# A linear-attention and rational feed-forward kernel: steps ordered by a whole-program table, loads held back, coefficients formed early

## Chip, cores, metric

One NeuronCore of one Trainium2 chip. The metric is the device time of one execution in microseconds, as the median of the runs; "span" is the length of the one profiled execution, some 1.5 to 2 us shorter. PE is TensorE, DVE VectorE, ACT ScalarE, POOL GpSimd, SP SyncE.

## The reference, cut to what matters

```python
# q, k, v, f_logit: (4, 8, 768, 48) float32
f = 1.0 / (1.0 + np.exp(-f_logit))
for t in range(S):
    state = f[:, :, t, :, None] * state + np.einsum('bhd,bhe->bhde', k[:, :, t], v[:, :, t])
    y[:, :, t] = np.einsum('bhd,bhde->bhe', q[:, :, t], state)
x = y.transpose(0, 2, 1, 3).reshape(3072, 384)
h = x @ w_in                                   # (3072, 2048)
P = a[0] + a[1] * h + a[2] * h**2 + a[3] * h**3
Q = 1.0 + np.abs(b[0]) * np.abs(h) + np.abs(b[1]) * h**2
out = (P / (Q + 1e-06)) @ w_out                # (3072, 384)
```

## The kernel before

The attention goes in chunks of 128 tokens; a *unit* is one chunk of two batches, 12 in all. Each unit feeds two *groups* of the feed-forward part (8 of 16 blocks of d_ff each), 24 groups in all. The order is set by hand: no scheduler reorders it, so each engine is given its instructions in the order in which the kernel names them. Steps: `a_ef` log of the gate, `a_cs` its running sum, `a_exp` the two decay factors A0 and A1, `a_mul` q and k times these, `a_T`/`a_Te` transposes and their copy (qkT), `a_sc`/`a_mask` scores, `a_sv`/`a_st` state, `a_y`/`a_ye` output, `a_x`/`a_xe` its transpose (xT); `m_h`/`m_y` h = x w_in and its cast, `m_sq`, `m_abs`, `m_u`, `m_ln`, `m_ex` the reciprocal of Q as exp(-ln), `m_p1` to `m_p3` the polynomial, `m_g` the product, `m_o`/`m_oe` the second matmul and its copy out.

```python
    def load(n):                      # one unit: f, k, q on SP's queue, v (cast to bf16) on GpSimd's
        ...
        for dst, src, eng in ((fn, f_logit, nc.sync), (kn, k, nc.sync),
                              (qn, q, nc.sync), (vn, v, nc.gpsimd)):
            for j in range(UB):
                eng.dma_start(out=dst[:, j], in_=src[...].rearrange("h t d -> t h d"))
# --- start (cut) ---
    a_mul(0)
    coefficients()
    for cast in casts:
        cast()
    load_w_in(2)
    load_w_in(3)
    load(2)
    ...
    load(3)
    for g in range(KF // WB):
        load_w_out(g)
# --- the loop, odd half period (cut) ---
            a_y(mf)
            a_ye(mf)
            if isu(mu):
                a_exp(mu, 1)
            m_u(gp_, 0)
            m_ln(gp_, 0)
            m_u(gp_, 1)
            m_ln(gp_, 1)
            a_st(mf)
            a_x(mf)
            a_xe(mf)
            if isu(mu):
                a_mul(mu)
                a_T(mu)
            m_ex(gp_)
            m_h(gh, 0)
            m_h(gh, 1)
            m_y(gh, 0)
            m_y(gh, 1)
            o_of(n, 0)
```

PSUM: a ring of two buffers for cs, hp (h) and u; one buffer for tp, scores and y; one each for the state and the op sums.

Of the kernel before, what the change touches and what calls it, by code (L numbers as in the profile page):

```python
# [14 lines left out]
PSUM = bass.MemoryType.PSUM  # L15


@with_exitstack
def kernel(
# [14 lines left out]
    C = 128  # L34
# [31 lines left out]

    U = consts.tile([C, C], BF16, name="U")
# [13 lines left out]
    sig = w_pool.tile([P, 4], F32, name="sig")  # L81
    w_in_sb = w_pool.tile([P, KD, d_ff], BF16, name="w_in_sb")
# [7 lines left out]
    def load(n):  # L90
        c, u = units[n]
        t0 = c * C
        fn = ld.tile([C, UB, H, D], F32, name="fn")
        kn = ld.tile([C, UB, H, D], F32, name="kn")
        qn = ld.tile([C, UB, H, D], F32, name="qn")
        vn = ld.tile([C, UB, H, D], BF16, name="vn")
        for dst, src, eng in ((fn, f_logit, nc.sync), (kn, k, nc.sync),
                              (qn, q, nc.sync), (vn, v, nc.gpsimd)):
            for j in range(UB):
                eng.dma_start(out=dst[:, j],  # L100
                              in_=src[u * UB + j, :, t0:t0 + C, :].rearrange("h t d -> t h d"))
        at_[n] = dict(fn=fn, kn=kn, qn=qn, vn=vn, qk=qkp[n % NQK], ls=lsp[n % NQK],
                      st=states[u], c=c, u=u)
# [23 lines left out]
    def a_mul(n):  # L127
        s = at_[n]
        nc.vector.tensor_mul(s["qk"][:, :, 0, :, 0:D], s["qn"], s["A", 0])  # L129
        nc.vector.tensor_mul(s["qk"][:, :, 1, :, 0:D], s["kn"], s["A", 1])  # L130
# [11 lines left out]

    def a_Te(n):
        s = at_[n]
        t = at.tile([P, UB, 2, HP, C], BF16, name="qkT")
        nc.vector.tensor_copy(t.rearrange("p j a b c -> p (j a b c)"),  # L146
                              s["tp"].rearrange("p j a b c -> p (j a b c)"))
        s["qkT"] = t
# [26 lines left out]
    def a_sc(n, j, ring=False):  # L175
        s = at_[n]
        sc = (psr if ring else psA).tile([C, 2, HP, C], F32, name="sc", tag="r" if ring else "A")
        for p in range(HP):
            for i in range(2):
                r = slice(64 * i, 64 * i + D)  # L180
                nc.tensor.matmul(sc[:, i, p, :], s["qkT"][r, j, 1, p, :], s["qkT"][r, j, 0, p, :],  # L181
                                 start=True, stop=True)
        s["sc", j] = sc
# [80 lines left out]

    def m_y(n, half):
        s = mg[n]
        if half == 0:
            s["y"] = ms.tile([P, W], BF16, name="hy")
        nc.scalar.copy(s["y"][:, half * W // 2:(half + 1) * W // 2],  # L269
                       s["hp", half].rearrange("p a n -> p (a n)"))  # L270
# [6 lines left out]
    def m_abs(n):  # L277
        s = mg[n]
        s["z"] = ms.tile([P, W], BF16, name="z")
        nc.vector.tensor_scalar(s["z"].bitcast(U16), s["y"].bitcast(U16), 0x7FFF, None,  # L280
                                op0=ALU.bitwise_and)
        m_u_early(n)
# [3 lines left out]
    def way_u(n):  # L286
        return "dve" if n >= NGR - 2 else "pe"

    def way_p(n):
        return "dve" if n >= NGR - 2 else "dma"  # L290

    def m_u(n, half):
        s = mg[n]
        way = way_u(n)
        if way == "pe":
            u = psr.tile([P, 2, NB], F32, name="u", tag="r")
            for i, src in enumerate((s["h2"], s["z"])):
                for e in range(2):
                    nc.tensor.matmul(u[:, e, :], ident,  # L299
                                     src[:, (half * 2 + e) * NB:(half * 2 + e + 1) * NB],  # L300
                                     start=(i == 0), stop=(i == 1))
            s["u", half] = u
        elif half == 0:
            m_u_early(n)

    def m_u_early(n):
        s = mg[n]
        if "u" in s:
            return
        s["u"] = s["z"]  # L310
        if way_u(n) == "dve":
            nc.vector.tensor_add(s["z"], s["z"], s["h2"])
        elif way_u(n) == "dma":
            nc.gpsimd.dma_start(out=s["z"], in_=s["h2"], accum_op=ALU.add)
        else:
            del s["u"]

    def m_ln(n, half):
        s = mg[n]
        if half == 0:  # L320
            s["lq"] = ms.tile([P, W], F32, name="lq", bufs=1)
        if ("u", half) in s:
            nc.scalar.activation(s["lq"][:, half * W // 2:(half + 1) * W // 2],  # L323
                                 s["u", half].rearrange("p a n -> p (a n)"), AF.Ln,
                                 scale=sig[:, 2:3], bias=1.0 + 1e-6)
        elif half == 0:
            nc.scalar.activation(s["lq"], s["u"], AF.Ln, scale=sig[:, 2:3], bias=1.0 + 1e-6)

    def part_of(t, part, parts):
        return t[:, part * W // parts:(part + 1) * W // parts]  # L330

    def m_ex(n, part=0, parts=1):
        s = mg[n]
        if part == 0:
            s["qi"] = ms.tile([P, W], BF16, name="qi")
        nc.scalar.activation(part_of(s["qi"], part, parts), part_of(s["lq"], part, parts), AF.Exp, scale=-1.0)  # L336

    def m_p1(n):

        s = mg[n]  # L340
        s["t"] = ms.tile([P, W], BF16, name="t", bufs=3)
        nc.vector.tensor_scalar(s["t"], s["y"], a_sb[:, 3:4], a_sb[:, 2:3], op0=ALU.mult, op1=ALU.add)
        nc.vector.tensor_mul(s["t"], s["t"], s["h2"])  # L343

    def m_p2(n):
        s = mg[n]
        s["pb"] = ms.tile([P, W], BF16, name="pb")
        nc.vector.tensor_scalar(s["pb"], s["y"], a_sb[:, 1:2], a_sb[:, 0:1], op0=ALU.mult, op1=ALU.add)  # L348

    def m_p3(n):  # L350
        s = mg[n]
        if way_p(n) == "dma":
# [31 lines left out]
    def m_oe(m, b, eng=None, queue=None):  # L384
        c, u = units[m]
        osb = ms.tile([P, DM], F32, name="osb", bufs=4)
        if eng is nc.vector:
            nc.vector.tensor_copy(osb, ops.pop((m, b)))
        else:
            nc.scalar.copy(osb, ops.pop((m, b)))  # L390
# [15 lines left out]
    def load_w_out(g):  # L406
        nc.gpsimd.dma_start(out=w_out_sb[:, g * WB:(g + 1) * WB, :],
                            in_=moe_w_out[g * WB * P:(g + 1) * WB * P, :].rearrange("(ko ki) n -> ki ko n", ki=P))


    load(0)
    nc.sync.dma_start(out=b_sb, in_=bass.AP(tensor=moe_b.tensor, offset=moe_b.offset,
                                            ap=[[0, P]] + list(moe_b.ap)))
    nc.sync.dma_start(out=a_sb, in_=bass.AP(tensor=moe_a.tensor, offset=moe_a.offset,
                                            ap=[[0, P]] + list(moe_a.ap)))
    make_upper_triangular(nc, U, 1.0, diag=True)
    make_identity(nc, ident)
    nc.vector.memset(zeros, 0.0)
# [10 lines left out]

    make_upper_triangular(nc, mask, 1.0, diag=True)  # L430
    casts = [load_w_in(0, False), load_w_in(1, False)]
    load(1)
# [13 lines left out]
    def isg(n):  # L446
        return 0 <= n < NGR

    def isu(m):
        return 0 <= m < NUN  # L450

    def o_of(n, part):

        m, b = divmod(n - NG - 1, NG)
        half = KF // 2
        if 0 <= m < NUN - 1:
            m_o(m, b, range(part * half, (part + 1) * half))

    def oe_of(n):
        m, b = divmod(n - NG - 1, NG)  # L460
        if 0 <= m < NUN - 1:
            m_oe(m, b)


    busy(12)
    a_ef(0)
    a_cs(0)
    a_exp(0, 0)
    a_exp(0, 1)
    a_mul(0)  # L470
    coefficients()
    for cast in casts:
        cast()
    load_w_in(2)
    load_w_in(3)
    load(2)
    busy(14)
    a_T(0)
    busy(6)
    a_Te(0)  # L480
    a_sc(0, 0)
    a_sc(0, 1, ring=True)
    a_sv(0)
    busy(3)
    a_al(0)
    a_mask(0, 0)
    a_mask(0, 1)
    a_y(0)
    busy(6)
    a_ye(0)  # L490
    a_st(0)
    a_x(0)
    busy(6)
    a_xe(0)
    a_ef(1)
    a_cs(1)
    m_h(0, 0)
    m_y(0, 0)
    a_exp(1, 0)
    m_h(0, 1)  # L500
    a_exp(1, 1)
    m_y(0, 1)
    a_mul(1)
    a_T(1)
    a_Te(1)
    load(3)
    for g in range(KF // WB):
        load_w_out(g)


    for n in range(0, NGR - NG):
        gp_, gn, gh = n - 1, n, n + 1
        if n % 2:
            mu, mf = (n + 3) // 2, (n + 1) // 2
            if isu(mu):
                a_exp(mu, 0)
            m_sq(gn)
            m_abs(gn)
            a_y(mf)
            a_ye(mf)  # L520
            if isu(mu):
                a_exp(mu, 1)
            m_u(gp_, 0)
            m_ln(gp_, 0)
            m_u(gp_, 1)
            m_ln(gp_, 1)
            a_st(mf)
            a_x(mf)
            a_xe(mf)
            if isu(mu):  # L530
                a_mul(mu)
                a_T(mu)
            m_ex(gp_)
            m_h(gh, 0)
            m_h(gh, 1)
            m_y(gh, 0)
            m_y(gh, 1)
            o_of(n, 0)
            if isu(mu):
                a_Te(mu)  # L540
            o_of(n, 1)
            oe_of(n)
            m_p1(gn)
            m_p2(gn)
# [120 lines left out]
```

## Time and profile before

| | before |
|---|---|
| time, median | 278.69 us (278.19 to 279.19, 2 runs) |
| span of the profiled run | 276.7 us |
| PE / DVE / ACT busy in the span | 84% / 77% / 75% |
| period of one unit in the middle | 19.78 us |
| PE / DVE / ACT busy per period | 18.2 / 16.9 / 17.2 us |

The prediction below shows the lines for these and how they are read (waits: engine, what waited, what for: us in total, times, longest). The waits are those of the kernel before between 110 and 190 us, four periods.

```profile
DVE scm L190 <- PE sc L181: 5.4, 4, 1.4
DVE qkT L146 <- PE tp L138: 5.1, 4, 1.3
```

In each period DVE too waits twice, 1.35 us for the scores and 1.27 us for the transposes. So PE and DVE each have two waits, and neither is full.

### The profile page before, as it was taken

What the parts mean: (1) busy time and instruction counts of PE and PEld (TensorE: products, weight loads), DVE (VectorE), ACT (ScalarE), POOL (GpSimd) and SP (SyncE); (2) the same over time, 40 slices, a digit from 0 to 9 for tenths busy, and PEclk for the clock granted to TensorE, in tenths of its full rate; (3) what the DMA queues carried; (4) which work ended last, traced back from release to release, by engine and by line L of the source; (5) the groups of instructions that cost most, each with busy time, mean ns of one, the idle gap of its engine ahead of it and who ended that gap; (6) DMA issues with size and microseconds to landing.
All of it is one profiled execution on the core that took longest, in us unless ns stands there. A gap on an engine that the chain in (4) does not pass through costs nothing.

```text
span 276.7 us, 5389 instructions
## 1 busy us (share of the span) xinstructions
PE 232.7 (84%) x2239; PEld 153.7 (56%) x2263; DVE 214.1 (77%) x235; ACT 207.9 (75%) x225; POOL 50.5 (18%) x64
## 2 busy tenths in 40 slices
PE   6587582596998998897997997997988989979993
PEld 2245451464664765664675675666656646646652
DVE  4280691499899878977978978978978988977991
ACT  4204568088979889799699699699799797976890
POOL 7086013013022112112112112112200201110000
PEclk9959977597999999999999999999999999999999
DMA  9999999899946967968959949849640540624002
GB/s 136 239 238 172 159 185 189 137 221 205 121 104 136 170 143 129 169 142 114 184 126 144 169 97 152 185 94 183 135 105 2 114 97 11 143 57 107 28 30 85
DMA packets 110488, 37.05 MB, mean 134 GB/s; under 512 B 100992, under 2 KB 106880, under 8 KB 110464
## 3 DMA queue, kind: packets, MB, share of 16 engines
q0 software_dynamic: 31040, 16.26, 43.6%
q1 hardware_dynamic: 79280, 20.26, 34.8%
q8 instruction: 17, 0.28, 0.4%
q10 hardware_dynamic: 144, 0.20, 0.2%
q14 instruction: 7, 0.06, 0.1%
HBM read 25.17 MB, written 4.72 MB: 108 GB/s over the span
## 4 chain that ended last, share of the span: by engine, by line
PE 52%; ACT 15%; SPq 11%; DVE 8%; DMA 6%; issue 6%; DVEq 0%; ACTq 0%
PE hp L261 20%; PE op L381 19%; SPq L100 10%; PE u L299 8%; DMA qn<-in_q_dram 6%; ACT A L123 4%; ACT ysb L217 3%; ACT lq L323 3%; ACT xT L248 3%; PE sc L181 2%; ACT osb L390 2%; DVE h L275 1%; ACT hy L269 1%; DVE gall L364 1%; PE sv L171 1%
## 5 line engine op out<-in xcount | busy, mean ns | idle before, releaser
L261 PE MATMUL hp<-xT,w_in_sb 128*128 128x256 bf16 x576 | 69.7, 279 | 8.7 <-ACT xT L248 7.1
L261 PEld LDWEIGHTS <-w_in_sb 128*128 128x128 bf16 x576 | 56.8, 100 | 18.3 <-issue 10.1
L381 PE MATMUL op<-w_out_sb,gall 128*128 128x384 bf16 x368 | 63.5, 326 | 1.0 <-ACT osb L390 0.6
L269 ACT CAST hy<-hp 128x1024 bf16<-128x1024 f32 x48 | 48.0, 1005 | 14.1 <-PE hp L261 14.0
L323 ACT ACTIVATE lq<-u,sig 128x1024 f32<-128x1024 f32 x44 | 47.9, 1114 | 5.6 <-PE u L299 4.4
L381 PEld LDWEIGHTS <-gall 128*128 128x128 bf16 x384 | 36.8, 98 | 24.8 <-DVE gall L364 0.8
L353 POOL DMA_DIRECT2D t<-pb x22 | 19.2, 875 | 147.7 <-DVE pb L348 147.7
L336 ACT ACTIVATE qi<-lq 128x2048 bf16<-128x2048 f32 (+1 forms) x25 | 46.1, 1847 | 0.1
L190 DVE TENSOR_TENSOR scm<-sc,mask 128x1024 bf16<-128x1024 f32 x24 | 29.2, 1220 | 11.7 <-PE sc L181 11.7
L299 PEld LDWEIGHTS <-ident 128*128 128x128 bf16 x176 | 16.5, 98 | 27.5 <-issue 12.3
L364 DVE TENSOR_TENSOR gall<-t,qi 128x2048 bf16<-128x2048 bf16 (+1 forms) x25 | 29.4, 1175 | 2.9 <-ACT qi L336 2.9
L275 DVE TENSOR_TENSOR h<-hy 128x2048 bf16<-128x2048 bf16 x24 | 29.3, 1220 | 2.8 <-ACT hy L269 1.9
L343 DVE TENSOR_TENSOR t<-t,h 128x2048 bf16<-128x2048 bf16 x24 | 29.4, 1225 | 0.8
L100 POOL DMA_DIRECT2D vn<-in_v_dram x24 | 22.3, 936 | 40.2 <-PE y L201 39.4
L129 DVE TENSOR_TENSOR qkp<-qn,A 128x768 bf16<-128x768 f32 x12 | 11.4, 950 | 23.2 <-DMA qn<-in_q_dram 15.0
L299 PE MATMUL u<-h,ident 128*128 128x512 bf16 x66 | 21.7, 383 | 8.0 <-ACT A L123 7.7
L299 PE MATMUL u<-z,ident 128*128 128x512 bf16 x88 | 26.6, 384 | 1.3 <-issue 0.2
L390 ACT COPY osb<-op 128x384 f32<-128x384 f32 x22 | 10.5, 479 | 22.2 <-PE op L381 22.2
L146 DVE COPY qkT<-tp 128x2048 bf16<-128x2048 bf16 x12 | 14.7, 1223 | 13.6 <-PE tp L138 13.6
L138 PE MATMUL tp<-ident,qkp 128*128 128x128 bf16 x192 | 14.2, 227 | 11.5 <-DVE qkp L129 9.8
L123 ACT ACTIVATE A<-cs 128x768 f32<-128x768 f32 x24 | 19.3, 811 | 0.6 <-PE cs L116 0.6
L348 DVE TENSOR_SCALAR pb<-hy,a_sb 128x2048 bf16<-128x2048 bf16 x24 | 19.4, 807 | 0.0
(59 smaller groups left out, 227.6 us busy)
## 6 DMA issues: line engine op xcount, KB each, us to landing
t<-pb POOLq DMA_DIRECT2D x22, 512.0 KB, 4.6
fn<-in_f_logit_dram SPq DMA_DIRECT2D x24, 192.0 KB, 4.7
kn<-in_k_dram SPq DMA_DIRECT2D x24, 192.0 KB, 5.3
qn<-in_q_dram SPq DMA_DIRECT2D x24, 192.0 KB, 5.1
out_dram<-osb SPq DMA_DIRECT2D x23, 192.0 KB, 2.8
vn<-in_v_dram POOLq DMA_DIRECT2D x24, 96.0 KB, 5.6
wst<-in_moe_w_in_dram SPq DMA_DIRECT2D x2, 768.0 KB, 5.8
w_out_sb<-in_moe_w_out_dram POOLq DMA_DIRECT2D x4, 384.0 KB, 17.3
```

What stands on the lines that cost most here:

```text
L100: eng.dma_start(out=dst[:, j], in_=src[u * UB + j, :, t0:t0 + C, :].rearrange("h t d -> t h d"))
L123: nc.scalar.activation(t.rearrange("p b h d -> p b (h d)"), s["cs"][:, :, 0:DM], AF.Exp, scale=(-1.0, 1.0)[i])
L190: nc.vector.tensor_mul(m, s["sc", j].rearrange("s i p t -> s (i p) t"), mb)
L261: nc.tensor.matmul(hp[:, e, :], w_in_sb[:, kk, f * P:(f + 1) * P], xT[:, kk, :], start=(kk == 0), stop=(kk == KD - 1))
L269: nc.scalar.copy(s["y"][:, half * W // 2:(half + 1) * W // 2], s["hp", half].rearrange("p a n -> p (a n)"))
L275: nc.vector.tensor_mul(s["h2"], s["y"], s["y"])
L299: nc.tensor.matmul(u[:, e, :], ident, src[:, (half * 2 + e) * NB:(half * 2 + e + 1) * NB], start=(i == 0), stop=(i == 1))
L323: nc.scalar.activation(s["lq"][:, half * W // 2:(half + 1) * W // 2], s["u", half].rearrange("p a n -> p (a n)"), AF.Ln, scale=sig[:, 2:3] ...
L336: nc.scalar.activation(part_of(s["qi"], part, parts), part_of(s["lq"], part, parts), AF.Exp, scale=-1.0)
L343: nc.vector.tensor_mul(s["t"], s["t"], s["h2"])
L364: nc.vector.tensor_mul(galls[m][:, lo:lo + w, :].rearrange("p a n -> p (a n)"), part_of(s["t"], part, parts), part_of(s["qi"], part, parts))
L381: nc.tensor.matmul(ops[m, b], galls[m][:, mm, b * C:(b + 1) * C], w_out_sb[:, mm, :], start=(mm == 0), stop=(mm == KF - 1))
```

## The change

Intent: let a search, not a hand-written loop, place every step of the whole program; issue each load only when those needed earlier are in; form the coefficients while the first loads are under way.

```diff
+STEPS = """
+    efl:0 cs:0 A1:0 A0:0 mk:0 mq:0 T:0 sv:0 Te:0 sc0:0 m0:0 sc1:0 m1:0 y:0 al:0 ye:0 st:0 efl:1 x:0 cs:1
+    ...
+    La1:0 vl:3 x:1 tb:0 mq:2 xe:1 T:2 zb:0 qb:0 ha1:1 Te:2 Ea:0 sb:0 sv:2 Pa:0 Ya1:1 ha0:1 efl:4 sc0:2
+    m0:2 ub0:0 Ya0:1 efl:3 ta:1 sc1:2 al:2 hb0:1 m1:2 ga:0 Lb0:0 y:2 qa:1 Yb0:1 cs:3 A0:3 st:2 A1:3
+    ...                                      (683 steps in all; ":n" is the unit, a/b the group)
+    Lb0:11 Oa:10 ob0:10 Pb:11 ob1:10 Eb:11 Ob:10 gb:11 oa0:11 oa1:11 Oa:11 ob0:11 ob1:11 Ob:11
+"""
+P_BY_DMA = {4, 5, ..., 21}     # before: 0 to 21; the rest of the sums t + pb are DVE adds
...
+    coefficients()             # before: behind a_mul(0)
     busy(12)
+    casts[0]()
+    load_v(1)
+    casts[1]()
     load_w_in(2)
     load_w_in(3)
+    def after(n):              # a 32-byte transfer on SP that reads what a load has written
+        src = (w_in_sb[0:1, 0, d_ff - 16:d_ff], w_out_sb[0:1, KF - 1, 0:16])[n]
+        nc.sync.dma_start(out=hold[0:1, n, :], in_=src)
+    after(0)                   # SP: nothing further before w_in has landed
     load(2)
+    nc.gpsimd.tensor_copy(hold[0:1, 2, :], at_[2]["qn"][0:1, UB - 1, H - 1, 0:16])
+    load_v(2)                  # POOL: nothing further before q of unit 2 has landed
     for g in range(KF // WB):
         load_w_out(g)
+    after(1)                   # SP: nothing further before w_out has landed
+    for token in STEPS.split():
+        key, n = token.split(":")
+        n = int(n)
+        steps[key](n)
+        if key == "mk" and n + 3 < NUN:
+            load(n + 3)
```

The two loads of the small vectors a and b go to ACT's queue. The last Exp, product and op sums are no longer split or interleaved as before.

## The prediction

> **What bounds the kernel now.** I read the page first: busy shares, the 40 slices, the chain that ended last.
>
> ```profile
> PE 232.7 (84%) x2239; PEld 153.7 (56%) x2263; DVE 214.1 (77%) x235; ACT 207.9 (75%) x225; POOL 50.5 (18%) x64
> PE   6587582596998998897997997997988989979993
> PEclk9959977597999999999999999999999999999999
> DMA  9999999899946967968959949849640540624002
> PE 52%; ACT 15%; SPq 11%; DVE 8%; DMA 6%; issue 6%; DVEq 0%; ACTq 0%
> ```
>
> No engine is full over the whole span, and the slices say why: the first nine or ten (6.9 us each) are another regime. There the DMA row is at 9 and PE is at 2 to 9, at a granted clock of 0.5 to 0.9. After it PE is at 8 to 9. So the table of windows comes next, with two windows at the end of the start stage and one from the middle (columns: from:to, length, then PE, PEld, DVE, ACT, POOL busy, clock, DMA share, GB/s).
>
> ```profile
> 40.00:50.00 10.00, 2.73 (x29) 1.49 (x29) 2.84 (x4) 6.88 (x7) 2.19 (x2) 0.77 1.26 180
> 50.00:70.00 20.00, 15.89 (x153) 10.89 (x156) 17.47 (x19) 12.65 (x14) 3.67 (x4) 0.77 1.04 194
> 129.50:149.00 19.50, 17.90 (x192) 12.18 (x193) 16.69 (x19) 16.93 (x20) 3.58 (x4) 1.00 0.87 147
> ```
>
> The reader is to see a hole at 40 to 50 us, then a slow-clock stage, then a stage in which three engines are nearly full together. The chain of waits names the hole, and the waits of the stretch from 110 to 190 us (four periods) name what PE still loses in the steady stage:
>
> ```profile
> 33.16 17.13 DMA qn<-in_q_dram
> ...
> 111.71 2.78 PE hp L261 x24
> ...
> 131.49 2.78 PE hp L261 x24
> ```
>
> ```profile
> PE u L299 <- ACT A L123: 3.3, 4, 0.8
> ...
> PE hp L261 <- ACT xT L248: 2.7, 4, 0.7
> ```
>
> The same step recurs after 131.49 - 111.71 = 19.78 us: the period of one unit (two batches by 128 tokens; there are 12 units, each with two groups of the feed-forward part, 24 groups in all). Scaled to it, PE is busy 17.90 x 19.78/19.5 = 18.2 us, ACT 17.2, DVE 16.9. PE waits 0.8 + 0.7 = 1.5 us a period, both times for ACT work that stands too late in ACT's order. That is nearly all of its idle 1.6 us. So the steady stage is PE with an order problem; the first 55 us are DMA.
>
> **What the Trainium skill says.** (1) "DMA: Bandwidth & Descriptors", section Issuing engines are not separate DMA queues: transfers started by different engines run on the same 16 DMA engines and interleave. The trace agrees: q of the third unit took 17.13 us to land beside the w_out loads of GpSimd, against a median of 5.1 us. So the order of issue does not protect an early load from a later one. (2) "TensorE: Matmul & The Clock Gate", Part 1: an idle TensorE falls to half clock and needs some 3.4 us of work to come back. The trace agrees in kind: after the hole, 24 hp matmuls took 3.85 us, against 2.78 later. (3) The same page, under Architectural detail: ACT and DVE queues are strict FIFO. The two repeated waits fit that; it makes one badly placed step hold all behind it.
>
> **The change, part by part.**
>
> (a) Held loads. Unit 2's loads of f, k and q now wait until w_in has landed; v of unit 2 and w_out wait for q of unit 2; units 3 and on wait for w_out. Read off the DMA view, f/k/q loads alone move at about 220 GB/s (50 to 60 us), the f32 w_in stage at 385, the cast loads at about 180. One unit's f, k, q are 6 x 192 KB = 1.18 MB, so 5.3 us; its v is half the bytes in equally many packets, about 2 us. Estimate, from those, for q of unit 2: start 2 + three units 16 + two v 4 + staged w_in 4 + cast w_in 4.4 + one held gap 2 = 32 to 34 us, not the 50.3 at which the q step waiting for it began. The hole at 43 to 50 goes. But the debt remains: then v and w_out (2 + 8.7 us) and a gap of 2 follow, so load 3 starts at about 46 and ends at 51, and f of unit 4 is there at 53 to 55. In the table ACT's step efl:4 stands ahead of efl:3 and of Ya0:1, so ACT, having done only about 23 us of work, comes to it at about 42 and must stand until f of unit 4 is in. PE has finished by then what it had finished before the change at 57 to 58 us. The head's gain is therefore not 16 us but about 57 - 53.5 = 3.5.
>
> (b) Coefficients. Nine small DVE instructions ran from 13.52 to 16.45 and delayed the first qkT copy from 14.5 to 16.36. They move under the wait for q. This is 1.9 us on the first unit's path, but the path then meets (a): worth 0 at the end.
>
> (c) Four adds t+pb go from DMA to DVE (groups 0 to 3). The same add on DVE at the end takes 1.23 us, spacing about 1.13: 4.5 us more of DVE, and 4 x 512 KB of accumulating transfer less. It falls in two periods whose DVE load becomes 16.9 + 2.3 = 19.2 us, above PE's 18.2: it costs about 1 us.
>
> (d) The order in the steady stage. Counts of matmuls are the same (the instruction order shows 4,528 rows on PE in both). What moves: in the table, between x:6 and the first h of unit 6 stand ub0:4, oa0:3, oa1:3, sc0:7 and both ua:5, so the wait for xT has over 5 us of other PE work over it; between the cs step and the u that takes its PSUM buffer stand op halves of 1.3 us each. Both 0.7 and 0.8 us waits can go. A finer mixing brings some others (ring of two PSUM buffers, in-order ACT), so I keep 0.6 of the 1.6: the period becomes 18.8. The stretch from 72.3 to 230.0 is eight periods: 8 x 0.98 = 7.8 us. In the last two units (230 to 270 us) PE idles 40 - 18.07 - 9.55 - 9.01 = 3.4 us; half of it, 1.5, is recovered.
>
> (e) The end. The last Exp and product are no longer in halves, and op of the last unit is ordered oa, Oa, ob. Before: the last half product ends at 270.20, PE at 272.54, copies at 273.65. After, on the same clock: product 0.5 us later at 270.7, then 24 matmuls x 0.163 (2.60 us for 16) = 3.9, then one copy of 0.48: 275.1. It costs 1.5 us.
>
> Sum: -3.5 + 0 + 1 - 7.8 - 1.5 + 1.5 = -10.3; 278.7 - 10.3 = 268.4. A searched order was presumably kept because it won, and my share kept in (d) is cautious, so I lean to 266.5.
>
> **The rivals.** *A new stall takes the head's place, fully.* Transfers with held gaps use the 16 engines less; if f of unit 4 lands at 58 or later, the head gives nothing, and the idle PE again restarts at half clock. For it: efl:4 before efl:3, and the gaps. Against it: four accumulating transfers are gone and nothing collides. It would make 270 to 272. *The head is a real gain.* If loads run at 250 GB/s, as in some slices of that window, f of unit 4 is there at about 48, and with the low-clock stage gone too the head gives 9 to 11 us: 257 to 260. *The steady stage does not move.* A table made for modelled durations may turn two clean waits into many small ones, with ACT (17.2) and DVE (16.9) both over 90% of an 18.5 us period. For it: DVE and ACT can delay PE at every PSUM hand-over. The period would stay at 19.5: 273 to 275. *The steady stage becomes PE-bound outright*, period 18.3: 4 us more than my sum, 262 to 263.
>
> **Range and chances.** The head spans -10 to +1, the steady stage -2 to -13, the rest about +1. Both extremes together are unlikely: 258 to 274 should hold it 8 times in 10, with 266.5 as the middle. Faster by over 2% means below 273.1: it takes only a third of the steady gain with a small head gain, or the reverse: 0.85. Within 2%: 0.12. Slower: 0.03, as nothing here adds over 5 us of work to any engine.
>
> **What would show it.** Right: q of unit 2 no longer waited for at 50 us; an ACT wait at the fifth ef for the DMA of f, 8 to 16 us long, ending at 51 to 57; the recurrence of a step of one unit to the next at 18.5 to 19.1 in the middle; PE waits on A and xT under 0.3 us a period; DVE with 4 more adds; about 6 us from the start of the last product with the Exp to the end of the last copy. Wrong: ACT reaching the fifth ef without a wait (head better, time near 258), a period at or over 19.5 (time near 274), or the clock low beyond 75 us.

## The result, and the profile after

| | before | after |
|---|---|---|
| time, median | 278.69 us (2 runs) | 267.69 us (267.52 to 267.85, 2 runs) |
| ratio, with 95% interval | | 0.9605 (0.953 to 0.968) |
| span | 276.7 | 265.7 |
| PE / DVE / ACT busy | 232.7 / 214.1 / 207.9 | 229.0 / 215.7 / 206.5 |

A ratio here is the mean time of one kernel's fast runs over that of the other's in the same rounds, so it is not quite the ratio of the medians. The total is 1.2 us from the prediction and 0.7 from its plain sum of 268.4. The parts are not so close. First the page of the changed kernel, its slices (6.6 us each) and the chain that ended last:

```profile
PE   6659947500879999999999999999999999999884
PEclk9986997955799999999999999999999999999999
DMA  9999659999995649699999299952350852624111
PE 67%; DMA 13%; SPq 7%; ACT 5%; POOL 4%; issue 2%; DVE 0%; ACTq 0%
```

From the thirteenth slice to the last three PE is at 9 without a break, where before it kept falling to 7 or 8 (the prediction, reading the row before as "at 8 to 9", passed over the 7s). But there is a deeper hole than before: PE at 0 in the ninth and tenth slices. The table of windows of the changed kernel, same columns as in the prediction, puts numbers on both:

```profile
50.00:60.00 10.00, 0.37 (x8) 0.29 (x8) 0.00 (x0) 0.00 (x0) 0.00 (x0) 0.61 1.53 169
60.00:70.00 10.00, 3.83 (x46) 2.63 (x46) 3.85 (x4) 6.25 (x8) 0.00 (x0) 0.53 1.43 187
150.00:169.50 19.50, 19.50 (x234) 13.62 (x233) 19.35 (x22) 18.36 (x22) 8.54 (x9) 1.00 1.25 185
```

PE did 0.37 us of work in the ten from 50 us, with DVE and ACT at zero, and restarted at a clock of 0.53 to 0.61. In the middle PE is busy for the whole window (a busy PE includes the end of each matmul as modelled), DVE for 99%. Between 110 and 190 us the list of waits of this kernel has not one of PE or DVE left; ACT's two largest there, over the whole 80 us, are small:

```profile
ACT y L334 <- PE hp L320: 1.6, 3, 0.7
...
ACT lq L367 <- PE u L354: 1.4, 3, 0.9
```

The timeline of ACT names the hole (start, length, ..., idle before and what ended it):

```profile
46.21 1.01 ACT L334 CAST y<-hp 128x1024 bf16<-128x1024 f32 x1 [2.10 <-PE hp L320]
63.50 0.84 ACT L166 ACTIVATE ef<-fn 128x768 f32<-128x768 f32 x1 [16.28 <-DMA fn<-in_f_logit_dram]
```

It is the fifth ef, that of unit 4 (`efl:4`), standing in the table ahead of `efl:3`. It waited 16.28 us for f of unit 4. The timeline of SP's queue says why that came so late, and the row of the DMA engines from 18 to 75 us (1.4 us a digit) shows what they did meanwhile:

```profile
27.77 0.62 SPq L492 DMA_DIRECT2D hold<-w_in_sb  x1
28.44 1.20 SPq L159 DMA_DIRECT2D fn<-in_f_logit_dram  x2
...
51.63 0.50 SPq L492 DMA_DIRECT2D hold<-w_out_sb  x1
52.23 2.26 SPq L159 DMA_DIRECT2D fn<-in_f_logit_dram  x2
...
58.03 1.75 SPq L159 DMA_DIRECT2D fn<-in_f_logit_dram  x2
```

```profile
DMA  9999950079996009999999999899999999999999
```

Two of the three holds drain the DMA engines: two digits of zero at about 27 to 30 us, ahead of unit 2's loads, and two more at about 37 to 40, ahead of w_out. At the third, at 51.6 us, the row stays at 9. The loads of unit 3 begin at 52 us, those of unit 4 at 58.

To split the gain, take the start of the square `m_sq` of a group as a milestone; it is one DVE instruction per group and stands in both traces.

| stretch, us | before | after | difference | predicted for it |
|---|---|---|---|---|
| start to group 4 | 77.29 | 85.32 | +8.0 | -2.5 (head -3.5, adds +1) |
| group 4 to 16 (6 units) | 117.89 | 110.70 | -7.2 | -5.9 (6 x 0.98) |
| group 16 to 23 (3.5 units) | 65.00 | 51.93 | -13.1 | -3.4 (2 x 0.98 + 1.5) |
| group 23 to the end | 16.5 | 17.8 | +1.2 | +1.5 |

The sum is -11.0. The cut at group 4 is not neutral: the table orders attention and feed-forward differently, and measured to the xT copy of unit 3 instead (91.09 before, 93.89 after) the head loses 2.8 us, not 8.0. Either way the head did not gain. It lost, and the rest gained about twice what was predicted.

The cut at group 16 is not neutral either: of the 13.1 us behind it, 7.1 are work that the table has already done by then (PE is busy 59.05 us there before, 51.93 after; it makes 16 transposes of q and k instead of 32). PE's idle time is the safer measure. From group 4 to 23 it falls from 15.5 us to 0.6, so by 15.0 us, about 9.0 of them before group 16 and 6.0 behind it.

### The profile page after: what moved, and what is told of

The parts are those of the page before. It is cut to its first block, busy times and chain, and to the rows that moved or that the text cites. A ratio compares the mean times of both kernels' runs of the same rounds, so it can differ in the third digit from the quotient of the medians.

```text
span 265.7 us, 5413 instructions
## 1 busy us (share of the span) xinstructions
PE 229.0 (86%) x2263; PEld 153.3 (58%) x2263; DVE 215.7 (81%) x237; ACT 206.5 (78%) x225; POOL 49.1 (18%) x61
## 4 chain that ended last, share of the span: by engine, by line
PE 67%; DMA 13%; SPq 7%; ACT 5%; POOL 4%; issue 2%; DVE 0%; ACTq 0%
PE hp L320 21%; PE op L419 20%; PE u L354 13%; SPq L159 7%; DMA w_in_sb<-in_moe_w_in_dram 4%; DMA w_out_sb<-in_moe_w_out_dram 3%; PE y L260 3%; PE tp L194 3%; PE sc L240 2%; DMA wst<-in_moe_w_in_dram 2%; DMA qn<-in_q_dram 2%; DMA kn<-in_k_dram 2%; ACT qi L372 1%; POOL vn L159 1%; PE xps L301 1%
## 5 line engine op out<-in xcount | busy, mean ns | idle before, releaser
L334 ACT CAST y<-hp 128x1024 bf16<-128x1024 f32 x48 | 48.4, 1016 | 10.2 <-PE hp L320 9.7
L372 ACT ACTIVATE qi<-lq 128x2048 bf16<-128x2048 f32 x24 | 46.2, 1925 | 0.1
L391 POOL DMA_DIRECT2D t<-pb x18 | 16.4, 910 | 134.3 <-DVE t L382 113.9
L377 DVE TENSOR_SCALAR t<-y,a_sb 128x2048 bf16<-128x2048 bf16 x24 | 20.1, 837 | 18.9 <-ACT y L334 18.8
L402 DVE TENSOR_TENSOR gall<-t,qi 128x2048 bf16<-128x2048 bf16 x24 | 29.2, 1219 | 1.0 <-ACT qi L372 0.9
L339 DVE TENSOR_TENSOR h<-y 128x2048 bf16<-128x2048 bf16 x24 | 29.2, 1217 | 0.4 <-ACT y L334 0.4
L354 PE MATMUL u<-h,ident 128*128 128x512 bf16 x88 | 26.2, 380 | 0.6 <-ACT A L180 0.6
L166 ACT ACTIVATE ef<-fn 128x768 f32<-128x768 f32 x12 | 10.2, 854 | 19.9 <-DMA fn<-in_f_logit_dram 19.9
L385 DVE TENSOR_SCALAR pb<-y,a_sb 128x2048 bf16<-128x2048 bf16 x24 | 20.3, 845 | 0.0
L186 DVE TENSOR_TENSOR qkp<-kn,A 128x768 bf16<-128x768 f32 x12 | 11.4, 951 | 10.1 <-ACT A L180 7.0
L344 DVE TENSOR_SCALAR z<-y 128x2048 uint16<-128x2048 uint16 x24 | 17.3, 721 | 0.9 <-ACT y L334 0.9
```

Source lines behind the costliest of these rows:

```text
L334: nc.scalar.copy(part_of(tile_of(n, "y"), half), mg[n]["hp", half].rearrange("p a n -> p (a n)"))
L339: nc.vector.tensor_mul(s["h2"], s["y"], s["y"])
L354: nc.tensor.matmul(u[:, e, :], ident, src[:, (half * 2 + e) * NB:(half * 2 + e + 1) * NB], start=(i == 0), stop=(i == 1))
L372: nc.scalar.activation(part_of(tile_of(n, "qi"), part, parts), part_of(mg[n]["lq"], part, parts), AF.Exp, scale=-1.0)
L385: nc.vector.tensor_scalar(tile_of(n, "pb"), mg[n]["y"], a_sb[:, 1:2], a_sb[:, 0:1], op0=ALU.mult, op1=ALU.add)
L402: nc.vector.tensor_mul(galls[m][:, lo:lo + w, :].rearrange("p a n -> p (a n)"), part_of(s["t"], part, parts), part_of(s["qi"], part, parts))
```

## The experiments

Each ran beside the kernel before on its own chip, e1 to e8 on one and e9 to e12 on another; the median of the kernel before was 278.3 to 278.5 us on both. All twelve gave the correct result.

| run | what | us, median | ratio to before (95%) |
|---|---|---|---|
| (after) | the change | 267.69 | 0.9605 (0.953 to 0.968) |
| e1_no_holds | change without the three holds | 261.88 | 0.9407 (0.938 to 0.943) |
| e2_before_with_holds | before, plus the three holds | 275.79 | 0.9906 (0.988 to 0.993) |
| e3_w_out_last | change, only w_out held, behind unit 3 | 250.38 | 0.9006 (0.898 to 0.904) |
| e4_ef4_late | change, `efl:4` moved back | 264.28 | 0.9479 (0.944 to 0.952) |
| e5_before_two_waits | before, PE's two waits taken away | 280.51 | 1.0103 (1.003 to 1.017) |
| e6_tail_halves | e3 with the end of before | 249.37 | 0.8960 (0.894 to 0.898) |
| e7_p_all_dma | e3, all sums t + pb by DMA | 262.14 | 0.9421 (0.939 to 0.945) |
| e8_coef_late | change, coefficients late | 267.39 | 0.9612 (0.959 to 0.964) |
| e9_before_dve_moves | before, DVE's two waits taken away | 278.79 | 1.0014 (0.996 to 1.007) |
| e10_before_both_moves | before, all four taken away | 277.43 | 0.9951 (0.992 to 0.998) |
| e11_more_dve | e6 + 6.5 us of DVE work | 253.46 | 0.9103 (0.907 to 0.914) |
| e12_more_pe | e6 + 7.6 us of PE work | 258.18 | 0.9263 (0.924 to 0.929) |

### The head: e1 to e4

My theory: the new order earns everything, and the holds cost, because the DMA engines stand idle behind them and f of unit 4 is the first load to feel it. The rival: the holds are what protects the head, and the stall is only what is left.

**e1: no holds.**

```diff
-    after(0)
     load(2)
-    nc.gpsimd.tensor_copy(hold[0:1, 2, :], at_[2]["qn"][...])
     load_v(2)
     ...
-    after(1)
```

> The changed kernel with all three holds of the loads taken out (two small transfers on SP, one small copy on GpSimd); order table, coefficients and adds stay. Theory A (the new order earns everything, the holds cost time because the DMA engines stand idle behind them at about 25 to 29 and 34 to 40 us): the fifth ef stops waiting for f at about 54 to 57 us instead of 63.5 or earlier, and the time is 257 to 262. Rival B (the holds earn the head and protect q of unit 2; without them the old hole comes back): q of unit 2 is again there only at about 50 us, PE loses the clock, and the time is at or above that of the changed kernel, 267 to 271.

261.88 us: at the upper end of the theory's range, 5.8 us less than with the holds. The lines of ACT and DVE in the timeline show what remains:

```profile
57.44 0.84 ACT L166 ACTIVATE ef<-fn 128x768 f32<-128x768 f32 x1 [3.80 <-DMA fn<-in_f_logit_dram]
...
47.13 0.96 DVE L186 TENSOR_TENSOR qkp<-qn,A 128x768 bf16<-128x768 f32 x1 [3.43 <-DMA qn<-in_q_dram]
```

The wait for f of unit 4 falls from 16.28 to 3.80 us. The rival has its part: q of unit 2 is again late, used at 47.1 us instead of 41.3, and w_out now runs beside it. The holds do guard q; they take more than they give.

**e2: the holds on the old order.** The same three holds put into the kernel before (the w_out loads moved ahead of `load(3)`).

> The kernel before with only the holds of the loads added (w_in, then unit 2, then w_out, then unit 3); its order of steps stays. Theory A says that in this order, which asks for f of unit 3 before that of unit 4, the hole at 43 to 50 us goes but the waits return at unit 3, so that it gains some: 270 to 276; the period in the middle stays at 19.78 us. Rival B (the holds are a large part of the gain): 265 to 269. If the holds alone do harm: above 279.

275.79 us, at the top of the range. The period in the middle is 19.77 us, unchanged. With e1 this makes a square: all of the change but the holds -16.4 us, the holds alone -2.5, both -11.0. Had the two effects added up, both would have given -19.0. In the old order ACT asks for f of unit 3 first, and only at 54.4 us (it then waits 6.38 us); the table asks for f of unit 4 at 47.2 us. That fits the holds helping a little there and hurting here.

**e3: w_out truly last.** w_out is first read at 82 us in the changed kernel; f of unit 4 is wanted at 47. So the holds before unit 2 and unit 3 go, and w_out waits for q of unit 3:

```diff
-    after(0)
     load(2)
-    nc.gpsimd.tensor_copy(hold[0:1, 2, :], at_[2]["qn"][...])
     load_v(2)
-    for g in range(KF // WB):
-        load_w_out(g)
-    after(1)
     ...
+        if key == "vl" and n == 3:
+            nc.gpsimd.tensor_copy(hold[0:1, 2, :], at_[3]["qn"][0:1, UB - 1, H - 1, 0:16])
+            for g in range(KF // WB):
+                load_w_out(g)
```

> The changed kernel with loads truly in order of first use: no hold before unit 2 or unit 3, and w_out (first read at 82 us) held until q of unit 3 has landed. Theory A: f of unit 4 is there at 40 to 45 us, before ACT comes to it at 47, so the wait of 16.3 us goes whole and the time is 250 to 254. Rival B (the stall is put off, to k and q of units 3 and 4 or to w_out): 256 to 262, with a DMA wait of some microseconds later than 47 us. Rival C (the head is bound by bytes, whatever the order): 263 or more.

250.38 us, the theory's range: 10% below the kernel before. ACT's timeline and the page's slices (6.2 us each) of this run:

```profile
46.87 0.84 ACT L166 ACTIVATE ef<-fn 128x768 f32<-128x768 f32 x1 [1.83 <-DMA fn<-in_f_logit_dram]
```

```profile
PE   7668967677999999999999999999999999999884
PEclk9995999999999999999999999999999999999999
```

The wait is 1.83 us, since f came at 46.9 and not at 40 to 45, and the clock does not fall again after the fourth slice. The milestones say that nothing else moved: start to group 4 takes 68.46 us (85.32 in the changed kernel), group 4 to 16 110.39 (110.70), 16 to 23 51.93 (51.93). All of the gain over the changed kernel is in the head. Rival C, a head bound by bytes in whatever order, is refuted: the same bytes were moved. Of the 17.3 us between the changed kernel and this one, taking the holds away is worth 5.8 (e1); the other 11.5 come from loading w_out behind unit 3.

**e4: the step moved, the holds kept.**

```diff
- ... Ya1:1 ha0:1 efl:4 sc0:2 ...
- ... Lb1:0 vl:4 Yb1:1 mk:3 ...
+ ... Ya1:1 ha0:1 sc0:2 ...
+ ... Lb1:0 vl:4 Yb1:1 efl:4 mk:3 ...
```

> The changed kernel, holds and all, with one step of ACT moved: the ef of unit 4 no longer stands ahead of that of unit 3 but behind the casts of group 1 of unit 1. If the place of that step in ACT's strict order is what the 16.3 us wait costs, the wait shrinks to that for f of unit 3 (there at about 57 us): 261 to 264. If the loads of unit 3 bind by themselves (k and q at 60 to 65 us), only 1 to 3 us come: 265 to 267.

264.28 us, just above the first range. ACT now waits at the ef of unit 3, 12.51 us until 59.76. So the place of one step in ACT's strict order cost about 3.4 us; most of the stall is the lateness of the loads, which e3 cured.

### The middle: e5, e9, e10

The prediction put the table's gain in the middle down to two waits of PE. **e5** takes away these two alone in the hand-written loop.

```diff
             a_exp(mu, 0)
+            a_exp(mu, 1)
         ...
         m_ex(gp_)
+        o_of(n, 0)              # moved, with the rest, from behind m_y(gh, 1)
+        a_Te(mu)
+        o_of(n, 1)
+        oe_of(n)
         m_h(gh, 0)
         m_h(gh, 1)
```

> The kernel before with two moves alone in every odd half period: the second exp of the A pair goes ahead of the mask stage, and the op matmuls go ahead of the hp matmuls, so that PE has work while xT is copied. Theory P (the prediction: the table's gain in the middle is these two repeated PE waits of 0.8 and 0.7 us): the two waits vanish, the period falls from 19.78 to 18.2 to 18.6 us, and the time to 266 to 270. Rival M (the gain comes from mixing all steps; taking the two waits away lets ACT or a PSUM hand-over wait instead): the period stays at 19.2 to 19.9, 274 to 280.

It is no faster (280.51 us, by a little above Rival M's range; its four runs scatter from 278.9 to 282.8), and the period, from one xT copy to the next, is 19.66 us. Yet both waits are gone from the list of waits between 110 and 190 us. These are there instead:

```profile
DVE h L275 <- ACT hy L269: 4.8, 4, 1.2
...
DVE qkT L146 <- PE tp L138: 4.7, 5, 0.9
...
PE sc L181 <- DVE scm L190: 3.2, 4, 0.8
```

Now DVE waits for the cast of h, and PE for the mask product. The theory of the prediction falls here. I formed another: DVE's own two waits set the period. **e9** takes those away in DVE's order alone (`m_p1`, `m_p2`, `m_p3` go ahead of `a_Te`; `m_g` goes between the two masks).

> The kernel before with two moves in DVE's order alone: in odd half periods t, t*h2 and pb go ahead of the qkT copy, in even ones the gall product goes between the two mask products. Theory D (new, after the two PE waits were taken away for nothing: the period of 19.78 us is DVE's 16.9 us of work plus its own two waits, 1.35 for the scores and 1.27 for the transposes): both DVE waits shrink below 0.3 us and the period falls to 17.3 to 18.6, time 262 to 270. Rival L (a loop through several engines; every single cure opens the next wait): the period stays above 19.2, 273 to 280.

278.79 us, and a period of 19.77. The two DVE waits no longer appear in the list; in their place, from the same stretch of its waits:

```profile
DVE h L275 <- ACT hy L269: 7.4, 8, 1.1
...
DVE gall L364 <- ACT qi L336: 3.6, 4, 0.9
...
PE u L299 <- ACT A L123: 3.3, 4, 0.8
...
PE hp L261 <- ACT xT L248: 2.7, 4, 0.7
```

PE's two waits, which this run left alone, stand at their old size to the tenth. That fits PE setting the pace in this version, with DVE only waiting elsewhere. **e10** makes both sets of moves.

> The kernel before with the DVE moves and the PE moves together: no PE wait for A and xT, no DVE wait for transposes and scores. Theory D: as with the DVE moves alone or a little better, 17.2 to 18.3 us a period, 258 to 268. Rival L: still 19 or more, 272 to 280. If each set alone gives nothing and both together give most of the table's 2.5 us: the loop went through both engines, 260 to 268.

277.43 us, a period of 19.37: 0.4 of the 1.6 us for which PE stood idle in each period. Apart from POOL, which has time to spare, the list of waits from 110 to 190 us leads with one wait of DVE, and the chain that ended last shows the loop it belongs to:

```profile
DVE h L275 <- ACT hy L269: 8.2, 4, 2.0
```

```profile
130.38 2.63 PE hp L261 x24
...
133.04 1.02 ACT hy L269
134.08 1.23 DVE h L275
...
138.62 1.15 DVE scm L190
...
139.81 0.40 PE sc L181 x8
140.21 2.71 PE op L381 x16
```

h on PE, its cast on ACT, the block of DVE products for the feed-forward, the mask behind them, then scores and op on PE, and round again. In this loop, written in blocks, each engine does the work of one group in one piece, and whichever of the four waits was cured, the loop closed through another engine. Rival L holds. That the table breaks such loops by mixing steps of several groups is what is left as explanation; it fits that the table has hardly any of these waits, but which of its moves are needed I have not separated.

### The limit of the table: e11, e12

Both start from e6 and repeat an instruction whose result does not change: in **e11** the product pb of one group of each of units 2 to 10 on DVE, in **e12** the 16 transposes of each of units 3 to 11 on PE.

> The best version so far (w_out last, end in halves; 249.4) with one DVE instruction done twice, pb of the second group of units 2 to 10: 9 x 0.72 = 6.5 us more of DVE, same result. If DVE is the bound in the table's steady stage (it shows 20.00 of 20 us): 253 to 256. If DVE has slack and PE is the bound: 249 to 251.

> The best version so far with the 16 transposes of units 3 to 11 done twice, same result: 9 x 16 x 53 ns = 7.6 us more of PE. If PE is the bound: 255 to 257.5. If PE has slack: 249 to 251.5. If both this and the doubled DVE instruction cost their length, the table has balanced the two engines to the same period.

6.5 us more of DVE cost 4.1 us (253.46 against 249.37), which is in the range given for DVE as the bound; 7.6 us more of PE cost 8.8 us (258.18), above the range given for PE. (e6 ran on the other chip; by the ratios the two costs are 4.0 and 8.4 us.) Both engines cost something, and one average hides two stages. Windows of e6 without added work, of 20 us each:

```profile
110.00:130.00 20.00, 19.84 (x224) 14.05 (x226) 20.00 (x22) 19.04 (x22) 3.64 (x4) 1.00 1.10 178
170.00:190.00 20.00, 19.95 (x189) 13.48 (x190) 18.35 (x20) 19.09 (x22) 1.69 (x2) 1.00 0.25 61
```

DVE is full at first and has 1.65 of 20 us to spare later; PE is full in both. The milestones say the same. A doubled pb lasts 1.65 us in the trace of e11 against 0.80 for a single one, so each adds 0.85 us. From group 5 to group 14 (158 us in e6) e11 falls behind e6 by 4.4 us, with five doubled pb on the way: their full length. From there to group 23 four more add nothing: the delay goes from 4.2 to 3.1 us. In e12 the delay grows all the way, to 7.2 us at group 14 and 8.95 at group 23. So up to about 160 us the table keeps PE and DVE both full, and added work of either costs its length; after that PE alone is the bound. The windows from 110 to 130 us of e11 and e12, in this order, show the loaded engine full and the other one pushed back:

```profile
110.00:130.00 20.00, 19.13 (x213) 13.65 (x215) 19.96 (x23) 19.04 (x22) 3.65 (x4) 1.00 1.13 190
```

```profile
110.00:130.00 20.00, 19.89 (x240) 15.21 (x241) 18.85 (x21) 18.15 (x21) 3.65 (x4) 1.00 0.96 187
```

### Small parts: e6, e7, e8

**e6** gives e3 the end of the kernel before: last Exp and product in halves, first halves of both op sums ahead, the two last copies on ACT and DVE.

> The version with w_out loaded last, with the end of the kernel before put back: last Exp and last product in halves, first halves of both op sums ahead of the product, the two last copies on two engines and two queues. If the table's end costs what the prediction put on it: 1.5 to 3 us less, so 247.5 to 249 against 250.4. If the end is bound by something else: within 0.5 us.

249.37 against 250.38 us: 1.0 us less, between the two ranges. The last copy ends at 244.63 us in its trace and at 245.68 in that of e3, 1.05 us apart, though the interval of its ratio (0.894 to 0.898) only touches that of e3. It is the fastest version: 10.4% below the kernel before and, by the two ratios, 6.7% below the change.

**e7** puts the four early adds back on accumulating transfers (`P_BY_DMA = {0, 1, 2, 3, 4, ...}`), again on e3.

> The version with w_out loaded last, with the four adds of groups 0 to 3 back on accumulating transfers. Theory DVE (in the stage from 50 to 90 us DVE shows 9 to 10 of 10 and is the bound, as the prediction's term of 1 us for the adds says): 1 to 4 us less, 246.5 to 249.5. Theory PE or DMA (PE is the bound, or the transfers delay loads): 0 to 3 us more.

262.14 us: 11.8 us more, and neither range had it. The list of waits from 20 to 110 us has the cause:

```profile
DVE gall L402 <- DMA t<-pb: 10.7, 1, 10.7
```

The two transfers were issued at 47.6 us, right behind the four w_out loads on GpSimd's queue. The slowest took 16.5 us to land (the median of all 22 is 5.8), a gall product stood still for them, and then the rest: start to group 4 takes 79.12 us against 68.46 in e3, and nothing else moved by more than 0.5. So these adds on DVE keep the product from waiting for a transfer issued behind w_out. Whether the queue or the engines shared with all loads made it late was not separated, and what the adds themselves cost DVE (20.00 of 20 us busy in the windows of e3 from 70 to 130 us) is not shown.

**e8** puts the coefficients back behind `a_mul(0)` in the changed kernel.

> The changed kernel with the nine small coefficient instructions put back behind the first products of q and k. The prediction put them at 1.9 us on the path of unit 0 and at 0 in the whole, because the start waits for loads further on: 267.2 to 268.2 as the changed kernel. If the start is a chain of work: 269 to 270.

267.39 against 267.69 us, with overlapping intervals: nothing, as predicted.

## Why the prediction was right in the total and wrong in its parts

- **What bounds the kernel.** Right: the first 55 us are loads, and the middle is order. The DVE waits of 1.35 and 1.27 us stood in the same answer as the two PE waits and were passed over.
- **(a) Held loads.** The mechanism was right, and it is the one that decides the head: ACT at `efl:4` waits for f of unit 4, and the hole only moves. The size was off, even in sign. I had q of unit 2 at 32 to 34 us, load 3 starting at 46 and f of unit 4 at 53 to 55. They were at 37.5, 52.2 and 63.5. Each stretch of its sum was too short. w_in had landed at 27.8 us (about 25 in the sum). From there to q of unit 2 took 9.7 us (7.3), v and w_out with their gaps 14.7 (12.7), and from the start of load 3 to f of unit 4 11.3 (about 8). Part of this is the gap of a hold: 2 us in the sum, where the engines twice stood idle for about 3 us. Part is the rate: 220 GB/s in the sum, where the window of 50 to 60 us from which it was read has a mean of 174. So the sign "ending at 51 to 57" failed too. -3.5 became a loss of 2.8 to 8.0, by milestone. The rival "a new stall takes the head's place, fully" is what happened, and worse than it was put. e1 and e3 show what it cost: without the holds 5.8 us come back, and with w_out behind unit 3 as well 17.3.
- **(b) Coefficients.** Right: 0 (e8).
- **(c) Adds on DVE.** The price of 1 us was not measured by itself, and what they save was missed: e7 shows 11.8 us in the version e3. That the same holds in the changed kernel was not run.
- **(d) The middle.** The number was near for groups 4 to 16: 110.70/6 = 18.45 us a unit against 18.8 predicted. The named step, "Both 0.7 and 0.8 us waits can go", was wrong as a cause: e5 takes both away and keeps 19.66. "I keep 0.6 of the 1.6" and "half of it, 1.5, is recovered" for the last units were the terms mis-sized: PE's idle time went almost wholly, 15.0 us of 15.5, where the prediction had 9.3. The rival "PE-bound outright, period 18.3" was the better description (e12), with DVE equally full up to about 160 us (e11).
- **(e) The end.** Predicted +1.5; the milestone says +1.2, and undoing it gave 1.0 (e6).

So the sum was right by luck, as two large errors cancelled: the head was 5 to 10 us worse than worked out, by milestone, and all that follows it as much better.

The Trainium skill, page "Perfetto Trace Analysis", section Identifying the Most-Contended Engine, says that matmul busy time is a poor measure of how close PE is to its limit and points to the busy share of weight loads. This case does not tell the two apart: from 110 to 190 us PE's busy share rose from 92% to 100% and that of its weight loads from 63% to 69%, a rise by a factor of 1.09 and of 1.10.

## What to carry to other kernels

A hold that waits for a load to land can drain the DMA engines (two of three did here), so order the issue of loads by first use and hold back only the one that is needed last. In a loop written in blocks, do not value an ordering change by the waits it removes: remove one alone and see whether the period moves. And where a total agrees with its prediction, check the parts at milestones, since errors of 5 to 10 us can cancel, as they did here, and check whether work has moved across the milestone.

## What the Trainium skill lacked or had wrong

- "DMA: Bandwidth & Descriptors", section Issuing engines are not separate DMA queues: it says that transfers interleave, but not what this costs. Here q of unit 2 took 17.1 us beside w_out against a median of 5.1, and w_out's own loads landed in 17.3 us (median, before) and 7.5 (after, held apart).
- The same page: no figure for what it costs to hold an issue back until an earlier load has landed. Two 32-byte transfers used as holds landed in 1.8 and 3.7 us, and around the first of them and the copy that holds w_out the engines stood idle for about 3 us each.
- The same page, section Queues, rings and completion order: no number for what a transfer pays behind large loads of its own queue. In e7 an accumulating transfer of 512 KB, issued behind four w_out loads of 384 KB on GpSimd's queue, landed in 16.5 us against a median of 5.8 (with other loads on the same engines).
- "Perfetto Trace Analysis": no value of the weight-load share at which PE is full. In this kernel it was about 68% (13.65 of 20 us on the average of the windows from 70 to 230 us of e6), where added PE work cost its full length, and 70% with that work added (e12); at 62 to 63% before, PE was not full.
